# Head-by-head k-v products on array halves, weight pairs in three pieces, and a second buffer for the last weight chunk

## Chip, core and metric

The kernel runs on one core of a Trainium2 chip. The metric is the device time of one launch in microseconds (us). Engines are named as in the profile: PE is TensorE's matrix products and PEld its weight loads, DVE is VectorE, ACT is ScalarE, POOL is GpSimd, SP is the engine whose queue issues every DMA of this kernel.

## What is computed

Linear attention without a softmax, an RMS norm by head, a gated two-matrix layer, and a second layer with softmax gating and a layer norm:

```python
kv = einsum('bhsd,bhse->bhde', k, v)            # b 4, h 8, s 576, d 64
out = einsum('bhsd,bhde->bhse', q, kv)
x = out / sqrt(mean(out * out, -1) + 1e-6) * g_norm       # -> 2304 x 512
g = (x @ w_a) * (x @ w_b)                                 # 512 -> 1536
y = g @ w_out                                             # 1536 -> 512
h = y @ w_in                                              # 512 -> 1024
solu = h * softmax(h)
out = layernorm(solu) * g_ln @ w_out2                     # 1024 -> 512
```

The weights arrive as 64-bit floats and are turned into pairs of 32-bit values (an upper and a lower half) on the chip.

## The kernel before

One Python program writes out the order of every engine's instructions: a planner (`Order`) keeps a clock per engine with fixed costs, and at each step the main loop picks what PE does next from what the plan says is ready. The costs (`od.pe(1.09, ...)`, `t_act`, `t_vec`, `tt`) decide order only. `tt` ("VG") goes to DVE or POOL, whichever the plan says ends first. DMAs are issued by SP in program order, so a DMA that waits for a buffer holds back all later ones.

**Attention** (`front`, `back`). For each batch b and pair of heads p, `att_kv` multiplies k and v over the 576 tokens: four products of 128 rows and one tail of 64 rows, each 128 x 128, though only the two 64 x 64 blocks on the diagonal (one for each head) are used. ACT copies these into `bd`. The k-v buffers are two (`R_KV`), so the load of pair p + 2 waits for pair p's products. `att_1` multiplies q by `bd`, and DVE, ACT and POOL scale it. `att_2` transposes a tile of 128 tokens (line 785) and multiplies it by the constant matrices `m1`, `m2` (line 809), which give the sums and differences of token halves and rows that the next stage needs. Tokens are in three groups g of 2 x 288, 2 x 416 and 2 x 448; groups 0 and 1 pass through line 809, and group 2 gets its sums later in `third_group`.

**The two products x @ w_a and x @ w_b** (`Set`, line 926). For each of 12 chunks f of 128 columns and each group g, seven products of block sums (`PROD`, in the order `SEQ`) replace eight (Strassen-Winograd), each of 6 instructions on upper and lower halves. A chunk's weights go through `decode` (five DVE operations on two buffers), `gather`, `sums` into the stage buffer `wst` (part of `mx`; one buffer, `R_ST`), and `make_w`: ACT casts the upper half into `aw` (line 548), and DVE or POOL subtracts to get the lower half (line 270, as all of `tt`). There are two `aw` slots (`R_W`). `make_w` works in two pieces, 512 columns (rows 0 and 1 of the seven, for P1 and P2) and 1280 (all others). Chunks from 2 on are decoded only after `third_group` is done (`EARLY`). The last two chunks run groups 0 and 1 first: (10,0), (10,1), (11,0), (11,1), then (10,2), (11,2). Between them the 12 chunks of w_out and later matrices ("late" chunks) are decoded too; 11 of these are put away in DRAM meanwhile (`IN_AB`).

**The rest** (lines 1110 to 1154): g @ w_out, then h, the softmax and layer norm, and the last product.

Of the kernel before, what the change touches and what calls it, by code (L numbers as in the profile page):

```python
# [9 lines left out]
F32 = mybir.dt.float32  # L10
# [13 lines left out]
NF1 = DF1 // P  # L24
# [3 lines left out]
SC = 4  # L28
# [31 lines left out]

PROD = {"P1": (0, 1), "P2": (1, 2), "P3": (6, 0), "P4": (3, 6), "P5": (4, 4), "P6": (5, 5), "P7": (2, 3)}
SEQ = ["P1", "P2", "P6", "P5", "P7", "P4", "P3"]
NOP = 7
IN_AB = 11
EARLY = 2
# [126 lines left out]
def attention_moe_moe_kernel(ctx: ExitStack, tc, kv_in, kv_tail, q_in, g_norm, w1, w_in, w_out2, g_ln, out):  # L194
# [3 lines left out]
    nc = tc.nc  # L198
# [8 lines left out]
    att = tc.alloc_tile_pool(name="att", bufs=1, side="left")  # L207
# [83 lines left out]
    mix = {}  # L291
    for n in (P, D):
        c = n // 2
        m1, m2 = (att.tile([P, 4, c], F32, tag=f"m{n}_{i}", name=f"m{n}_{i}") for i in range(2))
        i0, i1 = ident[:, 0:c], ident[:, c:2 * c]
        nc.vector.memset(m2, 0.0)
        nc.vector.tensor_copy(out=m1[:, 0], in_=i0)
        for r in (1, 3):
            nc.vector.tensor_tensor(out=m1[:, r], in0=i0, in1=i1, op=ALU.subtract)
        for d in (m1[:, 2], m2[:, 3]):  # L300
            nc.vector.tensor_tensor(out=d, in0=i1, in1=i0, op=ALU.subtract)
        nc.vector.tensor_tensor(out=m2[:, 0], in0=m2[:, 1], in1=i0, op=ALU.subtract)
        nc.vector.tensor_copy(out=m2[:, 2], in_=i0)
# [31 lines left out]
    n_load, n_late = [0, 0], [0]  # L335
# [30 lines left out]
    def can(r, k):  # L366
        return pick(r, k) is not None
# [46 lines left out]
    def decode_more():  # L414

        q, lq = dec_q
        while q and q[0] in arrived and can(R_UF, q[0]):
            k = q[0]
            if k[1] not in stage:
                if k[1] >= EARLY and not third[1] or not R_ST.ok():  # L420
                    break
                stage[k[1]] = [R_ST.take(), wst, 2]
            decode(q.pop(0))
        for k in list(lq):
            if k in arrived and can(R_UF, k) and (own() or place(k) is not None):
                lq.remove(k)
                decode(k)
# [97 lines left out]
    def make_w():  # L525

        while w_wait and R_W.ok():
            f, st = w_wait.pop(0)
            slot = w_at[f] = R_W.take()
            hi, lo = w_ops(slot % 2)  # L530
            src = st[1]
            rank = rank_of(("w", f, 0)) - 0.2
            w_left[f] = NG
            left = [2]
            for half in range(2):
                s = slice(512, WSZ) if half else slice(0, 512)
# [15 lines left out]

    left_of = {}
    def w_used(f):
        w_left[f] -= 1
        if not w_left[f]:
            R_W.give(w_at[f])
            for h in range(2):
                w_ready.pop((f, h))
            make_w()  # L560

    half = {}
# [90 lines left out]
    tiles = {(b, i): (n, g, c) for b, i, n, g, c in AT}  # L653
# [22 lines left out]
    def run_front():  # L676
        w, b, i = front.pop(0)
        if w == "kv":
            od.pe(1.09, lambda: att_kv(b, i))
        else:  # L680
            od.pe(0.88, lambda: att_1(b, i))

    def run_back():
        _, b, t, x, sx = back.pop(0)
        od.pe(0.44 if tiles[b, t][1] == 2 else 2.0, lambda: att_2(b, t, x, sx))

    def att_kv(b, p):
        (slot, t, _), tl = arrived.pop(("kv", b, p)), arrived["tail", b, 0][1]
        sp = R_PA.take()
        bank, ps = ps_tile()  # L690
        o = ps[:, 0:P]
        for c in range(SC):
            nc.tensor.matmul(  # L693
                o, lhsT=t[:, c * P:(c + 1) * P], rhs=t[:, (SC + c) * P:(SC + c + 1) * P], start=c == 0, stop=False
            )
        r0 = D * (p % 2)
        nc.tensor.matmul(
            o, lhsT=tl[r0:r0 + D, p // 2, 0:P], rhs=tl[r0:r0 + D, p // 2, P:2 * P], start=False, stop=True
        )
        bd = bds[b % 2, p]  # L700

        def done(t):
            R_PA.give(sp)
            bd_ready[b, p] = t

        od.chain([
            ("A", 0.25, lambda: nc.scalar.copy(out=bd[0:D, 0:D], in_=ps[0:D, 0:D])),
            ("A", 0.25, lambda: nc.scalar.copy(out=bd[D:P, D:P], in_=ps[D:P, D:P])),
            ps_done(bank),
            (None, 0, done),  # L710
        ], rank=b, t=od.now + 1.09 + 0.2)
# [46 lines left out]
    def t_sums(s, d):  # L758

        c = s.shape[-1]  # L760
        return [
            ("V", t_vec(4 * c), lambda: nc.vector.tensor_tensor(
                out=d[:, 0:4].rearrange("p (a k) c -> p a k c", k=2),
                in0=s[:, 0:2].unsqueeze(1).to_broadcast([P, 2, 2, c]),
                in1=s[:, 2:6].rearrange("p (a k) c -> p a k c", k=2), op=ALU.subtract)),
            ("V", t_vec(2 * c), lambda: nc.vector.tensor_tensor(
                out=d[:, 4:6], in0=s[:, 2:4], in1=d[:, 2:4], op=ALU.subtract)),
            ("V", t_vec(2 * c), lambda: nc.vector.tensor_tensor(
                out=d[:, 6:8], in0=s[:, 6:8], in1=d[:, 4:6], op=ALU.subtract)),
        ]  # L770

    def pair_ops(hi, lo, src):
# [4 lines left out]
    def att_2(b, t, x, sx):  # L777
        n, g, c0 = tiles[b, t]
        c = n // 2
        sp = R_PA.take()  # L780
        bank, ps = ps_tile()
# [5 lines left out]
        rank = 1 + b  # L787
# [33 lines left out]
        for bk, src, h, l, m, dt in (  # L821
# [20 lines left out]
    third = [False, False]  # L842
# [48 lines left out]
    class Set:  # L891
# [14 lines left out]
        def run(s):  # L906
# [371 lines left out]
    while order or sets:  # L1278
# [21 lines left out]
        if not now and order and len(sets) < (1 if att_left[0] else ACTIVE):  # L1300
            s = Set(*order[0])
# [4 lines left out]
        if now:  # L1306
            s = now[0]
# [17 lines left out]
    while todo_o:  # L1325
# [94 lines left out]
```

## Time and profile before

| | |
|---|---|
| median of 3 runs | 759.5 us (758.02 to 759.54) |
| profiled execution | 757.83 us, its span 755.9 us |
| PE busy | 720.0 us, 95% of the span |
| DVE, POOL, ACT busy | 485.9, 302.7, 256.4 us |
| mean granted TensorE clock | 0.989 |

PE's busy time is modelled up to the end of each product, so it is not the share of its best speed. A granted clock of 1.00 is 2.4 GHz and 0.50 is 1.2 GHz. The rows further down are whole lines of the profile; "x8" counts instructions, and one 32-bit product is two of them.

### The profile page before, as it was taken

Reading aid. Unit: us, or ns where it says so; the run is one execution under the profiler, and the core shown is the slowest. Engines: PE = TensorE matmul, PEld = TensorE weight load, DVE = VectorE, ACT = ScalarE, POOL = GpSimd, SP = SyncE. Lnnn points to the kernel's source line nnn. Section 1 sums busy time; section 2 is a strip of 40 time slices with the busy share of each in tenths; the row PEclk is TensorE's granted clock in tenths of the full one; section 3 lists DMA queues with packets and bytes.
Section 4 is the critical chain, followed back from the end, with each engine's and each line's share of the span. In section 5 each row is a group of like instructions: output and inputs, shape, how many; then the busy total and the mean of one; then the engine's idle time right before and its main releaser. Section 6 shows DMA issues by size and latency. Waiting matters only on the chain.

```text
span 755.9 us, 10032 instructions
## 1 busy us (share of the span) xinstructions
PE 720.0 (95%) x3760; PEld 635.0 (84%) x3760; DVE 485.9 (64%) x726; ACT 256.4 (34%) x446; POOL 302.7 (40%) x287
## 2 busy tenths in 40 slices
PE   6989999799999999997989999999999999999997
PEld 5888898799899999897977788788888888988886
DVE  2857668989998899985586989733340165055361
ACT  1434554332433423432334444322232123213222
POOL 0454555654555544654167752612213222120110
PEclk9979999999999999999999999999999999999999
DMA  7165501443444534431878561211112101200101
GB/s 246 72 254 175 188 16 51 156 160 116 158 172 150 174 126 146 161 143 39 294 272 287 167 204 62 70 42 43 55 42 71 49 15 43 63 1 14 29 15 42
DMA packets 36336, 86.64 MB, mean 115 GB/s; under 512 B 4416, under 2 KB 12352, under 8 KB 36288
## 3 DMA queue, kind: packets, MB, share of 16 engines
q1 hardware_dynamic: 36288, 86.00, 33.8%
q8 instruction: 29, 0.48, 0.2%
q14 instruction: 19, 0.16, 0.1%
HBM read 61.35 MB, written 24.64 MB: 114 GB/s over the span
## 4 chain that ended last, share of the span: by engine, by line
PE 79%; DVE 9%; DMA 3%; POOL 3%; issue 2%; ACT 2%; SPq 0%; POOLq 0%; DVEq 0%; ACTq 0%
PE ps L926 26%; PE ps L1152 9%; PE ps L1154 9%; PE ps L1153 9%; PE ps L1110 5%; PE ps L1111 5%; PE ps L1112 5%; PE ps L809 3%; PE ps L723 3%; PE ps L693 2%; PE ps L1227 2%; PE ps L785 1%; POOL mx L270 1%; DVE mx L460 1%; DMA kv<-in_kv 1%
## 5 line engine op out<-in xcount | busy, mean ns | idle before, releaser
L926 PE MATMUL ps<-a,aw 128*128 128x288 f32 (+2 forms) x1512 | 274.3, 341 | 14.7 <-POOL aw L270 7.9
L926 PEld LDWEIGHTS ps<-a,aw 128*128 128x128 f32 x1512 | 256.6, 189 | 30.2 <-POOL aw L270 8.6
L270 POOL TENSOR_TENSOR gy<-mx,gy 128x512 fp32r<-128x512 f32 (+1 forms) x43 | 50.0, 1163 | 96.4 <-ACT gy L1081 93.0
L1198 DVE TENSOR_REDUCE mx<-ps 128x1 f32<-128x1024 f32 x18 | 22.0, 1221 | 82.5 <-PE ps L1154 82.3
L1110 PE MATMUL ps<-gy,a 128*128 128x512 f32 (+1 forms) x192 | 70.9, 369 | 2.3 <-DVE aw L1136 1.4
L1111 PE MATMUL ps<-gy,a 128*128 128x512 f32 (+1 forms) x192 | 69.7, 363 | 0.0
L1112 PE MATMUL ps<-gy,a 128*128 128x512 f32 (+1 forms) x192 | 69.7, 363 | 0.0
L944 ACT COPY gg<-ps 128x288 f32<-128x288 f32 (+2 forms) x72 | 34.4, 479 | 101.4 <-PE ps L926 97.8
L1152 PE MATMUL ps<-a,aw 128*128 128x512 f32 (+1 forms) x178 | 67.9, 381 | 0.0
L1153 PE MATMUL ps<-a,aw 128*128 128x512 f32 (+1 forms) x178 | 67.8, 381 | 0.0
L1154 PE MATMUL ps<-a,aw 128*128 128x512 f32 (+1 forms) x178 | 67.8, 381 | 0.0
L1000 POOL TENSOR_TENSOR gg<-gg,t 128x288 f32<-128x288 f32 (+2 forms) x36 | 41.4, 1150 | 58.0 <-DVE gg L998 57.9
L270 POOL TENSOR_TENSOR mx<-mx 128x512 f32<-128x512 f32 (+2 forms) x45 | 57.7, 1287 | 6.5 <-DVE mx L270 2.0
L751 POOL TENSOR_TENSOR r<-r,mhalf 128x8 f32<-128x8 f32 (+1 forms) x20 | 34.5, 1734 | 50.8 <-DVE r L740 50.6
L270 POOL TENSOR_TENSOR mx<-f,u 128x512 f32<-128x512 f32 x24 | 31.8, 1327 | 49.8 <-DVE u L469 48.5
L1081 ACT CAST gy<-mx 128x512 fp32r<-128x512 f32 (+1 forms) x48 | 27.2, 568 | 67.0 <-PE ps L1112 54.8
L1237 DVE TENSOR_TENSOR aw<-ps,aw 128x1024 fp32r<-128x1024 f32 x13 | 15.9, 1224 | 44.3 <-ACT aw L1236 44.2
L1199 ACT ACTIVATE mx<-ps,mx 128x1024 f32<-128x1024 f32 x18 | 20.1, 1118 | 69.0 <-DVE mx L1198 69.0
L1110 PEld LDWEIGHTS ps<-gy,a 128*128 128x128 f32 x192 | 36.3, 189 | 8.4 <-DVE aw L1136 1.8
L1112 PEld LDWEIGHTS ps<-gy,a 128*128 128x128 f32 x192 | 36.2, 189 | 5.7
L1111 PEld LDWEIGHTS ps<-gy,a 128*128 128x128 f32 x192 | 36.3, 189 | 5.3
L1152 PE MATMUL ps<-a 128*128 128x512 f32 x99 | 38.8, 392 | 1.3 <-DVE a L1237 1.3
(120 smaller groups left out, 1307.4 us busy)
## 6 DMA issues: line engine op xcount, KB each, us to landing
raw<-in_w SPq DMA_DIRECT2D x25, 512.0 KB, 4.2
mx<-gd SPq DMA_DIRECT2D x48, 256.0 KB, 2.7
kv<-in_kv SPq DMA_DIRECT2D x16, 512.0 KB, 3.3
mx<-in_w SPq DMA_DIRECT2D x11, 512.0 KB, 3.4
lscw<-mx SPq DMA_DIRECT2D x11, 512.0 KB, 2.6
a<-lscw SPq DMA_DIRECT2D x11, 512.0 KB, 6.8
gd<-gg SPq DMA_DIRECT2D x12, 448.0 KB, 2.5
gd<-gg SPq DMA_DIRECT2D x12, 416.0 KB, 3.0
```

The lines of the kernel that those rows point to most:

```text
L270: lambda e=e: e.tensor_tensor(out=out, in0=in0, in1=in1, op=op) for e in (nc.vector, nc.gpsimd)))
L751: ("G", 1.75, lambda: nc.gpsimd.tensor_tensor(out=r[0:n], in0=r[0:n], in1=mhalf[0:n], op=ALU.pow)),
L926: nc.tensor.matmul(o, lhsT=a[:, k], rhs=b[:, kt], start=first and kt == m == 0, stop=kt == 1 and m == 2, skip_group_check=not first,)
L944: od.chain([("A", t_act(s.n, True), lambda: nc.scalar.copy(out=dst(), in_=ps)), (None, 0, done)], t=t)
L1000: ("G", t_pool(s.n), lambda: nc.gpsimd.tensor_tensor(out=d, in0=d, in1=t3, op=ALU.mult)),
L1081: ("A", t_act(n), lambda t=t, gh=gh: nc.scalar.copy(out=gh, in_=t)),
L1110: nc.tensor.matmul(o, lhsT=wh[:, s], rhs=gh, start=f == 0, stop=False)
L1111: nc.tensor.matmul(o, lhsT=wh[:, s], rhs=gl, start=False, stop=False)
L1112: nc.tensor.matmul(o, lhsT=wl[:, s], rhs=gh, start=False, stop=f == NF1 - 1)
L1152: nc.tensor.matmul(o, lhsT=ah, rhs=bh, start=first, stop=False)
L1153: nc.tensor.matmul(o, lhsT=ah, rhs=bl, start=False, stop=False)
L1154: nc.tensor.matmul(o, lhsT=al, rhs=bh, start=False, stop=last)
```

## The change

`att_kv` makes the products head by head: 64 columns of k as weights and 64 of v, head 0 into partitions 0 to 63 (the left half of the array's columns) and head 1 into partitions 64 to 127, in turn: 10 products of 64 x 64 in the place of 5 of 128 x 128 (the two blocks that nobody read are no longer made); each head's sum stands in the columns 0 to 63 of the bank. `m2` loses its row of zeros (four blocks become three), for which the rows of the sums are numbered anew. `make_w` works in three pieces of 512, 768 and 512 columns, each with its own flag. Where the stage buffer is taken, the last chunk (11) may use another part of `mx`, if 11 late chunks have been started and the buffers that lie there are free. The planner's cost of a k-v product goes from 1.09 to 0.75, that of `att_2` from 2.0 to 1.9.

```diff
-PROD = {... "P4": (3, 6), "P5": (4, 4), "P6": (5, 5), "P7": (2, 3)}
+PROD = {... "P4": (3, 5), "P5": (4, 6), "P6": (5, 4), "P7": (2, 3)}
...
-        m1, m2 = (att.tile([P, 4, c], F32, tag=f"m{n}_{i}", name=f"m{n}_{i}") for i in range(2))
+        m1, m2 = (att.tile([P, 4 - i, c], F32, tag=f"m{n}_{i}", name=f"m{n}_{i}") for i in range(2))
...
-                if k[1] >= EARLY and not third[1] or not R_ST.ok():
+                if k[1] >= EARLY and not third[1]:
                     break
-                stage[k[1]] = [R_ST.take(), wst, 2]
+                if R_ST.ok():
+                    stage[k[1]] = [R_ST.take(), wst, 2]
+                elif k[1] == NF1 - 1 and n_late[0] >= IN_AB and R_RAW.ok(2) and R_UF.ok(2) and R_UF.ok(3):
+                    R_RAW.take(2), R_UF.take(2), R_UF.take(3)
+                    stage[k[1]] = [None, mx[:, 1792:3584], 2]
+                else:
+                    break
...
-            for half in range(2):
-                s = slice(512, WSZ) if half else slice(0, 512)
+            for half, s in enumerate((slice(0, 512), slice(1024, WSZ), slice(512, 1024))):
...
-        o = ps[:, 0:P]
-        for c in range(SC):
-            nc.tensor.matmul(
-                o, lhsT=t[:, c * P:(c + 1) * P], rhs=t[:, (SC + c) * P:(SC + c + 1) * P], start=c == 0, stop=False
-            )
...
+        for c in range(SC + 1):
+            for h in range(2):
+                o = ps[h * D:(h + 1) * D, 0:D]
+                if c < SC:
+                    k, v = (t[:, x * P + h * D:x * P + (h + 1) * D] for x in (c, SC + c))
+                else:
+                    k, v = (tl[r0:r0 + D, p // 2, x * P + h * D:x * P + (h + 1) * D] for x in range(2))
+                nc.tensor.matmul(o, lhsT=k, rhs=v, start=c == 0, stop=c == SC)
...
-                o = pt[:, kt * 4 * c:(kt + 1) * 4 * c]
...
+                o = pt[:, kt * 4 * c:kt * 4 * c + m.shape[-1]]
...
-            half = 0 if p in ("P1", "P2") else 1
+            half = {"P1": 0, "P2": 0, "P6": 1, "P5": 1}.get(p, 2)
```

The order moves on all engines up to the end of the line 926 stage; behind it PE's order is unchanged. Two places follow. In the names, `gg1_2` is the result tile of chunk 1 and group 2, `t31_2` its third buffer, `aw_80` the finished weights, `mx` the stage and late buffers. Lines of the changed kernel are shifted (457 to 475 were 451 to 469, 965 to 1008 were 957 to 1000).

The first place is the start of chunk 2. DVE before:

```order
L985 TENSOR_TENSOR gg1_2_1035<-ps_94,gg1_2_1035 128x448
L270 TENSOR_TENSOR mx_144<-mx_144 128x2x256
L998 TENSOR_TENSOR gg1_2_1035<-ps_94,gg1_2_1035 128x448
L460 SCALAR_TENSOR_TENSOR mx_144<-mx_144 128x512
L465 TENSOR_SCALAR mx_144<-mx_144 128x512
L469 SCALAR_TENSOR_TENSOR mx_144<-mx_144 128x512
L270 TENSOR_TENSOR aw_80<-mx_144,aw_80 128x1280
```

DVE now, at the same place:

```order
L270 TENSOR_TENSOR mx_142<-mx_142 128x256
L466 SCALAR_TENSOR_TENSOR mx_142<-mx_142 128x512
L471 TENSOR_SCALAR mx_142<-mx_142 128x512
L986 TENSOR_TENSOR t31_2_1213<-ps_94,t31_2_1213 128x448
L475 SCALAR_TENSOR_TENSOR mx_142<-mx_142 128x512
L993 TENSOR_TENSOR gg1_2_1139<-ps_94,gg1_2_1139 128x448
L1006 TENSOR_TENSOR gg1_2_1139<-ps_94,gg1_2_1139 128x448
L270 TENSOR_TENSOR aw_80<-mx_142,aw_80 128x512
L270 TENSOR_TENSOR aw_80<-mx_142,aw_80 128x768
```

The lower half of the first piece (512 columns), which POOL made before (its rows are not shown), now stands on DVE, behind the last two sums of set (1,2) and behind a late chunk's operations.

The second place is the start of chunk 11 on POOL. Before:

```order
L270 TENSOR_TENSOR mx_144<-mx_144 128x256
L270 TENSOR_TENSOR mx_144<-mx_144 128x2x256
L270 TENSOR_TENSOR mx_144<-mx_144 128x256
L1000 TENSOR_TENSOR gg10_1_2771<-gg10_1_2771,t310_1_2841 128x416
L270 TENSOR_TENSOR aw_80<-mx_144,aw_80 128x512
L1000 TENSOR_TENSOR gg11_0_2867<-gg11_0_2867,t311_0_2922 128x288
```

POOL now:

```order
L270 TENSOR_TENSOR mx_142<-f0_147,u0_145 128x512
L270 TENSOR_TENSOR mx_142<-f1_148,u1_146 128x512
L1008 TENSOR_TENSOR gg9_2_2751<-gg9_2_2751,t39_2_2844 128x448
L270 TENSOR_TENSOR mx_142<-mx_142 128x256
L270 TENSOR_TENSOR aw_80<-mx_142,aw_80 128x512
L1008 TENSOR_TENSOR gg10_0_2820<-gg10_0_2820,t310_0_2895 128x288
L270 TENSOR_TENSOR aw_80<-mx_142,aw_80 128x512
L1008 TENSOR_TENSOR gg10_1_2888<-gg10_1_2888,t310_1_2964 128x416
```

Chunk 11's gathers, sums and lower halves stood behind the end of (10,1); they now stand around the end of (9,2) and ahead of the end of (10,1).

## Rows read from the trace of the kernel before

**Rows 1.** The page: busy time by engine; the chain that ended last, by engine.

```profile
PE 720.0 (95%) x3760; PEld 635.0 (84%) x3760; DVE 485.9 (64%) x726; ACT 256.4 (34%) x446; POOL 302.7 (40%) x287
PE 79%; DVE 9%; DMA 3%; POOL 3%; issue 2%; ACT 2%; SPq 0%; POOLq 0%; DVEq 0%; ACTq 0%
```

**Rows 2.** Waits of PE: us in total, times, longest.

```profile
PE ps L926 <- POOL aw L270: 7.9, 3, 3.8
PE ps L926 <- DVE aw L270: 1.4, 2, 1.1
```

**Rows 3.** Timeline, first 24 us: start, us, engine, instruction, [idle before <- releaser].

```profile
1.65 4.84 SPq L352 DMA_DIRECT2D kv<-in_kv  x2
4.05 2.08 PE L693 MATMUL ps<-kv 128*128 128x128 f32 x8 [4.05 <-DMA kv<-in_kv]
6.78 2.07 PE L693 MATMUL ps<-kv 128*128 128x128 f32 x8
18.45 5.58 PE L723 MATMUL ps<-bd,q 128*128 128x128 f32 x28 [1.04 <-DMA q<-in_q]
```

**Rows 4.** Windows: length, busy PE, PEld, DVE, ACT, POOL, clock, DMA share, GB/s.

```profile
0.00:10.00 10.00, 5.95 (x22) 5.05 (x23) 3.00 (x24) 2.06 (x5) 0.72 (x7) 1.00 0.54 188
10.00:20.00 10.00, 8.07 (x30) 6.43 (x30) 2.78 (x4) 1.53 (x7) 0.00 (x0) 1.00 0.92 323
40.00:50.00 10.00, 10.00 (x44) 9.10 (x44) 1.32 (x4) 3.80 (x9) 4.60 (x5) 0.50 0.96 360
50.00:60.00 10.00, 9.46 (x67) 8.60 (x66) 8.66 (x16) 4.67 (x11) 4.34 (x3) 1.00 0.20 77
60.00:70.00 10.00, 10.00 (x68) 9.06 (x67) 8.82 (x18) 3.73 (x10) 4.24 (x4) 1.00 0.75 262
```

**Rows 5.** Timeline, PE around a later k-v product and a transpose of 64 columns.

```profile
87.43 1.06 PE L693 MATMUL ps<-kv 128*128 128x128 f32 x8
88.42 0.48 PE L697 MATMUL ps<-tail 64*128 64x128 f32 x2
88.83 0.66 PE L785 MATMUL ps<-ident,x 128*128 128x128 f32 x4
...
98.08 0.46 PE L785 MATMUL ps<-ident,x 64*128 64x64 f32 x4
98.47 1.06 PE L926 MATMUL ps<-a,aw 128*128 128x288 f32 x6
```

**Rows 6.** The chain that ended last, from 28 to 47 us: start, us, what.

```profile
28.17 1.73 PE ps L809 x8
...
36.36 3.25 DMA kv<-in_kv
...
39.75 1.96 PE ps L693 x8
...
44.67 2.00 PE ps L693 x8
```

**Rows 7.** Timeline, the start of chunk 2.

```profile
143.74 0.61 DVE L998 TENSOR_TENSOR gg<-ps,gg 128x448 f32<-128x448 f32 x1
...
146.11 1.45 POOL L270 TENSOR_TENSOR aw<-mx,aw 128x512 fp32r<-128x512 f32 x1
146.47 1.63 DVE L469 SCALAR_TENSOR_TENSOR mx<-mx 128x512 f32<-128x512 uint32 x1
...
147.61 12.60 PE L926 MATMUL ps<-a,aw 128*128 128x288 f32 x69 [3.83 <-POOL aw L270]
```

**Rows 8.** Windows (columns as in the windows above) at the start of chunk 2.

```profile
144.00:148.00 4.00, 0.39 (x3) 0.39 (x4) 3.93 (x4) 1.78 (x2) 4.00 (x4) 1.00 0.56 218
...
150.00:152.00 2.00, 2.00 (x8) 1.95 (x8) 2.00 (x4) 0.68 (x2) 1.75 (x1) 0.50 0.38 152
```

**Rows 9.** Groups by line and form: DVE's lower half of 512 columns, xcount | busy, mean ns.

```profile
L270 DVE TENSOR_TENSOR aw<-mx,aw 128x512 fp32r<-128x512 f32 x4 | 4.7, 1179 | 0.6 <-ACT aw L548 0.6
```

**Rows 10.** Timeline, the start of chunk 11.

```profile
351.80 8.45 PE L926 MATMUL ps<-a,aw 128*128 128x288 f32 x54 [3.22 <-POOL aw L270]
```

More of the change, by code (lines that the diff above doesn't have):

```diff
@@ L53 @@
 YB = [(0, 512), (512, 512), (1024, 512), (1536, 512), (2048, 256)]
-PROD = {"P1": (0, 1), "P2": (1, 2), "P3": (6, 0), "P4": (3, 6), "P5": (4, 4), "P6": (5, 5), "P7": (2, 3)}
+PROD = {"P1": (0, 1), "P2": (1, 2), "P3": (6, 0), "P4": (3, 5), "P5": (4, 6), "P6": (5, 4), "P7": (2, 3)}
 SEQ = ["P1", "P2", "P6", "P5", "P7", "P4", "P3"]
@@ L293, in attention_moe_moe_kernel @@
         c = n // 2
-        m1, m2 = (att.tile([P, 4, c], F32, tag=f"m{n}_{i}", name=f"m{n}_{i}") for i in range(2))
+        m1, m2 = (att.tile([P, 4 - i, c], F32, tag=f"m{n}_{i}", name=f"m{n}_{i}") for i in range(2))
         i0, i1 = ident[:, 0:c], ident[:, c:2 * c]
-        nc.vector.memset(m2, 0.0)
         nc.vector.tensor_copy(out=m1[:, 0], in_=i0)
-        for r in (1, 3):
-            nc.vector.tensor_tensor(out=m1[:, r], in0=i0, in1=i1, op=ALU.subtract)
-        for d in (m1[:, 2], m2[:, 3]):
+        for d in (m1[:, 2], m1[:, 3]):
+            nc.vector.tensor_tensor(out=d, in0=i0, in1=i1, op=ALU.subtract)
+        for d in (m1[:, 1], m2[:, 2]):
             nc.vector.tensor_tensor(out=d, in0=i1, in1=i0, op=ALU.subtract)
-        nc.vector.tensor_tensor(out=m2[:, 0], in0=m2[:, 1], in1=i0, op=ALU.subtract)
-        nc.vector.tensor_copy(out=m2[:, 2], in_=i0)
+        nc.vector.tensor_scalar(out=m2[:, 0], in0=i0, scalar1=-1.0, scalar2=None, op0=ALU.mult)
+        nc.vector.tensor_copy(out=m2[:, 1], in_=i0)
         mix[n] = tuple(x.rearrange("p r c -> p (r c)") for x in (m1, m2))
@@ L533, in make_w @@
             w_left[f] = NG
-            left = [2]
-            for half in range(2):
-                s = slice(512, WSZ) if half else slice(0, 512)
+            for half, s in enumerate((slice(0, 512), slice(1024, WSZ), slice(512, 1024))):
                 n, x = s.stop - s.start, src[:, s]
@@ L542, in done @@
                     if not left_of[f]:
-                        R_ST.give(st[0])
+                        if st[0] is None:
+                            R_RAW.give(2), R_UF.give(2), R_UF.give(3)
+                        else:
+                            R_ST.give(st[0])
                         decode_more()
-                left_of[f] = 2
+                left_of[f] = 3
                 od.chain([
@@ L557, in w_used @@
             R_W.give(w_at[f])
-            for h in range(2):
+            for h in range(3):
                 w_ready.pop((f, h))
@@ L678, in run_front @@
         if w == "kv":
-            od.pe(1.09, lambda: att_kv(b, i))
+            od.pe(0.75, lambda: att_kv(b, i))
         else:
@@ L684, in run_back @@
         _, b, t, x, sx = back.pop(0)
-        od.pe(0.44 if tiles[b, t][1] == 2 else 2.0, lambda: att_2(b, t, x, sx))
+        od.pe(0.44 if tiles[b, t][1] == 2 else 1.9, lambda: att_2(b, t, x, sx))
     def att_kv(b, p):
@@ L690, in att_kv @@
         bank, ps = ps_tile()
-        o = ps[:, 0:P]
-        for c in range(SC):
-            nc.tensor.matmul(
-                o, lhsT=t[:, c * P:(c + 1) * P], rhs=t[:, (SC + c) * P:(SC + c + 1) * P], start=c == 0, stop=False
-            )
-        r0 = D * (p % 2)
-        nc.tensor.matmul(
-            o, lhsT=tl[r0:r0 + D, p // 2, 0:P], rhs=tl[r0:r0 + D, p // 2, P:2 * P], start=False, stop=True
-        )
+        r0 = D * (p % 2)
+        for c in range(SC + 1):
[3 more added lines that the diff above has]
+                    k, v = (t[:, x * P + h * D:x * P + (h + 1) * D] for x in (c, SC + c))
+                else:
+                    k, v = (tl[r0:r0 + D, p // 2, x * P + h * D:x * P + (h + 1) * D] for x in range(2))
+                nc.tensor.matmul(o, lhsT=k, rhs=v, start=c == 0, stop=c == SC)
         bd = bds[b % 2, p]
@@ L707, in att_kv @@
             ("A", 0.25, lambda: nc.scalar.copy(out=bd[0:D, 0:D], in_=ps[0:D, 0:D])),
-            ("A", 0.25, lambda: nc.scalar.copy(out=bd[D:P, D:P], in_=ps[D:P, D:P])),
+            ("A", 0.25, lambda: nc.scalar.copy(out=bd[D:P, D:P], in_=ps[D:P, 0:D])),
             ps_done(bank),
             (None, 0, done),
-        ], rank=b, t=od.now + 1.09 + 0.2)
+        ], rank=b, t=od.now + 0.75 + 0.2)
         R_KV.give(slot)
@@ L762, in t_sums @@
             ("V", t_vec(4 * c), lambda: nc.vector.tensor_tensor(
-                out=d[:, 0:4].rearrange("p (a k) c -> p a k c", k=2),
+                out=d.rearrange("p (a k) c -> p a k c", k=2)[:, 0:4:3],
                 in0=s[:, 0:2].unsqueeze(1).to_broadcast([P, 2, 2, c]),
@@ L766, in t_sums @@
             ("V", t_vec(2 * c), lambda: nc.vector.tensor_tensor(
-                out=d[:, 4:6], in0=s[:, 2:4], in1=d[:, 2:4], op=ALU.subtract)),
+                out=d[:, 2:4], in0=s[:, 2:4], in1=d[:, 6:8], op=ALU.subtract)),
             ("V", t_vec(2 * c), lambda: nc.vector.tensor_tensor(
-                out=d[:, 6:8], in0=s[:, 6:8], in1=d[:, 4:6], op=ALU.subtract)),
+                out=d[:, 4:6], in0=s[:, 6:8], in1=d[:, 2:4], op=ALU.subtract)),
         ]
```

## The prediction

> **What bounds the kernel.** I read the page first. PE is busy for 95% of the span, and the chain that ended last runs on PE for 79% of its length, with DVE, DMA and POOL sharing most of the rest [rows 1]. So a microsecond taken from PE is a microsecond gained only where PE is what ends last. The edits touch four places, and each has its own limit.
>
> The first 25 us belong to DMA. PE's first product waits 4.05 us for the first load, and at 18.45 it waits once more for q [rows 3]. The DMA engines are busy for 0.54 of the first 10 us and 0.92 of the next 10 [rows 4]. The early products are also slow: eight instructions take 2.08 us [rows 3], and the same eight take 1.06 us later [rows 5].
>
> Between 28 and 48 us the chain goes from PE to a load of k and v of 3.25 us, and back to k-v products of 1.96 and 2.00 us [rows 6]. The granted clock is 0.50 (1.2 GHz) from 40 to 50 [rows 4]. From 50 to 70 PE is busy again for nearly all the time, but DVE is busy for 8.66 and 8.82 us of each 10, so here two engines are near their limit [rows 4].
>
> In the stage of line 926, PE's waits for the lower half of the weights sum to 7.9 us on POOL (three, the longest 3.8) and 1.4 us on DVE [rows 2]. Two of them are large: 3.83 us before chunk 2 [rows 7] and 3.22 us before chunk 11 [rows 10].
>
> **The k-v product itself.** A product before is eight instructions of 128 columns and two for the tail. From the start at 87.43 to the next shape at 88.83 it takes 1.40 us [rows 5]. Line 809 gives a clean price: eight instructions of 256 columns in 1.73 us [rows 6], 0.216 each, 0.00084 us a column. So 128 columns cost 0.108 and 64 columns 0.054, both estimates. Eight of 128 make 0.86, and the tail starts at 88.42, 0.99 after the first; 0.13 is the switch to another shape. The tail's two make 0.22, and the next shape starts 0.41 later; 0.19 is the switch back [rows 5].
>
> After, a product is 20 instructions of 64 columns (16 and 4), in turn on the left and right half of the array. Nothing in this trace shows two halves at work together, so I bound it. If they work fully beside each other, it is 10 x 0.054 = 0.54, and with the switches, which grow to some 0.45 because the array is split, 0.99. If one follows the other, it is 20 x 0.054 + 0.45 = 1.53. If each costs what a transpose of 64 columns does, (98.47 - 98.08 - 0.13) / 4 = 0.065 [rows 5], it is 1.75. I take w = 1.10: nearly beside each other, with 0.11 for the first and last pieces, since the two halves write different partitions and need no result of each other. That saves 0.30 us at 2.4 GHz and 0.60 at 1.2 GHz.
>
> One rule speaks against this edit. The Trainium skill, page "TensorEngine Tiling (Array Packing)", section "Key Properties", says that changing the tiling mode drains the engine; the trace agrees, 0.13 and 0.19 at the two shape switches [rows 5]. The same section says that different tiles can load weights and multiply in parallel, which no run here shows yet; by it alone the product would be 0.99 and the sum below 1.7 us lower.
>
> Where these savings count:
>
> (a) Batch 0. The loads of pairs 2 and 3 wait for the buffers of pairs 0 and 1, so a shorter product lets SP issue them, and q behind them, sooner; DMA has room in the first 10 us (0.54) and PE waits for q at 18.45 [rows 3, 4]. Two products at the slow speed count: -1.2. Pairs 2 and 3 themselves lie behind their loads: 0.
>
> (b) Batch 1. Its first product stands ahead of the load of 3.25 in the chain (-0.3), and two stand in the chain at the clock of 0.50 [rows 4, 6]: -1.2. Together -1.5.
>
> (c) Batches 2 and 3. Eight products at 0.30 are 2.4. DVE is busy 87 and 88% there [rows 4]; I count 0.8 of it, -1.9.
>
> So a change of w weighs 2 x 2 + 1 + 2 x 2 + 8 x 0.8 = 15.4 times.
>
> **att_2.** Of the eight instructions of line 809, four go from 256 to 192 columns: 4 x 64 x 0.00084 = 0.216 us a tile. Four tiles of batch 0 stand in the chain [rows 6]: -0.86. Later six whole tiles and a half make 1.4; with the 0.8 of (c), -1.1. The setup of m2 loses a few DVE operations that lie under the first load's 4.05 us [rows 3]: 0, and a few tenths of a us if that cover went.
>
> **Start of chunk 2.** Before, POOL makes the lower half of the first piece from 146.11 to 147.56, and PE starts at 147.61 [rows 7]. Now DVE makes it, behind a late chunk's last decode operation and the last two sums of set (1,2), and DVE is already full: busy 3.93 of the 4 us from 144 to 148 [rows 8]. Before, DVE's last decode operation ended at 148.10 (146.47 + 1.63) [rows 7]. The two sums that stood ahead of it (0.61 each, as line 998) have moved behind it, another sum of 0.61 has moved in: 148.10 - 1.22 + 0.61 = 147.5. Then come the two sums, 1.22, and the lower half, 1.18 [rows 9]: 149.9, against 147.56. That is **+2.3**. If the planner's shift lets the earlier operations run sooner it is 0; if the six PE products that now precede the last results delay the sums, +3.5. The clock falls to 0.50 behind this wait before [rows 8] and should again, so that adds nothing. The other pieces (768, 512) come later than PE needs the first, and P1 and P2 use only the first.
>
> **Start of chunk 11.** The wait of 3.22 us [rows 10] stands there because the stage buffer is freed late, and then gathers, sums and lower half follow on POOL. With a second buffer they stand ahead of the end of (10,1), so only a normal gap stays: **-3.1**. At worst (the buffer's old users finish late) it is 0.
>
> **Other chunk starts.** The waits that remain, 7.9 + 1.4 - 3.83 - 3.22 = 2.25 us [rows 2], may go or grow; I take 0, and 1.5 either way. The 12 more casts and subtractions (three pieces for two) lie beside PE: ACT is busy 34%, POOL 40% [rows 1]. Behind the stage of line 926 PE's order is the same: 0.
>
> **The sum.** -1.2 - 1.5 - 1.9 - 0.86 - 1.1 + 2.3 - 3.1 = -7.4 us. The profiled execution took 757.83, so it would be 750.4; the median lies 1.7 above the profiled one, at 759.5, and I predict for a median **752.1**.
>
> **Rivals.** (R1) *The halves go one after another.* For it: no row shows them together, and the weights of each piece must be loaded as well (PEld is busy 84% [rows 1]). Against it: they share neither columns nor output partitions. Then w = 1.53, +0.13 x 15.4 = +2.0, and the other terms are -0.86 - 1.1 + 2.3 - 3.1 = -2.8: together -0.8, 758.7, no change that can be told.
>
> (R2) *DVE bounds the attention from 50 to 100 us.* For it: 8.66 and 8.82 of 10 [rows 4]; PE would only wait longer for the normalised tiles. Against it: PE itself has no idle time from 60 to 70. Then (c) and the later att_2 are worth nothing, 3.0 less: -4.4, 755.1.
>
> (R3, the other side) *Small pieces cost a fixed time.* For it: the transposes of 64 columns at 0.065 each [rows 5], while 64 columns should take 0.054. Against it: a transpose also waits for its operand. With w = 1.75 the k-v products cost +0.35 x 15.4 = +5.4, and with -2.8 it is +2.6: 762.1, slower. It decides (slower by 1.5 us) from w = 1.40 + (1.5 + 2.8) / 15.4 = 1.68, that is from 0.061 us a piece. Beside it, in a sentence by itself: the Trainium skill, page "TensorEngine Tiling (Array Packing)", section "Instruction Overhead", says that a product of one column takes as long as one of 60 and that no tiling should cut a dimension that is already small; 64 columns stand just above that, and no run here shows the floor.
>
> **How the numbers follow.** Forecast 0.57, R1 0.17, R2 0.16, R3 0.10. A measurement of this kernel can tell about 0.2% (1.5 us) from no change, so the forecast and R2 are faster, and with a part of R1, at its faster end, that is 0.79; the rest of R1 is the same, 0.11; R3 is slower, 0.10. The likeliest case alone has 746 to 756: w = 0.99 (-1.7), chunk 2 without loss (-2.3) and other starts (-1.5) towards one end, chunk 2 at +3.5 and other starts at +1.5 with a part of chunk 11's gain lost towards the other. The range runs from 745, a little below that, up to 759.5, which takes in R2 and R1 and leaves out R3.
>
> **What the profile will show.** If I am right, a k-v product at 2.4 GHz takes about 1.1 us to the next shape; the load of pair 2 of batch 0 is issued earlier and line 723 starts earlier than 18.45; line 809's groups take about 1.5 us; PE waits some 6 us before chunk 2, for DVE; and no wait of over 1 us stands before chunk 11. R1 shows as 1.5 us for the product, R3 as 1.7 or more, R2 as new idle time of PE between 50 and 100 with DVE as what ended it. The prediction fails if the shorter k-v work leaves PE with more idle time early and the granted clock stays at 0.50 for longer than from 40 to 50 [rows 4], or if the new piece order makes PE wait at chunk starts that had no wait before.

## Result and the profile after

The changed kernel is slower: a median of 767.9 us against 759.0, a ratio of 1.0111 with a 95% interval of 1.0063 to 1.0159. The forecast was 752.1, faster. The profiled execution took 767.73 us.

First the page of the changed kernel, the line that answers to [rows 1]:

```profile
PE 713.2 (93%) x3920; PEld 626.5 (82%) x3920; DVE 485.5 (63%) x725; ACT 258.3 (34%) x458; POOL 314.1 (41%) x298
```

PE has 6.8 us less work shown and the span is 9.7 us longer: the time is in waits. PE's waits, as in [rows 2], the largest:

```profile
PE ps L707 <- DMA kv<-in_kv: 11.4, 6, 4.0
PE ps L934 <- DVE t L986: 8.6, 9, 2.3
PE ps L934 <- ACT a L783: 4.8, 1, 4.8
...
PE ps L934 <- DVE aw L270: 1.9, 1, 1.9
...
PE ps L934 <- POOL aw L270: 1.4, 2, 1.0
```

Line 926 is now 934. What it waited for before, the lower half of the weights, has shrunk from 9.3 us to 3.3; in its place stand one wait of 4.8 us for the third group of tokens (line 783) and nine for a sum on DVE (line 986, which adds a product into `t`).

The edited products, in PE's timeline (the places of [rows 3] and [rows 5]):

```profile
4.05 1.12 PE L707 MATMUL ps<-kv 128*64 128x64 f32 x16 [4.05 <-DMA kv<-in_kv]
...
17.93 6.81 PE L731 MATMUL ps<-bd,q 128*128 128x128 f32 x30 [1.21 <-DMA q<-in_q]
...
28.25 1.68 PE L817 MATMUL ps<-m,x 128*128 128x256 f32 x8
29.76 0.60 PE L793 MATMUL ps<-ident,x 128*128 128x128 f32 x4
...
52.46 0.69 PE L707 MATMUL ps<-kv 128*64 128x64 f32 x16
53.07 0.33 PE L707 MATMUL ps<-tail 64*64 64x64 f32 x4
53.33 1.16 PE L731 MATMUL ps<-bd,q 128*128 128x128 f32 x8
```

A k-v product at 2.4 GHz takes 53.33 - 52.46 = 0.87 us to the next shape, where 1.40 stood before; the eight instructions of att_2 (now line 817) take 1.51 in place of 1.73. So both edits of the attention did on PE what they should, the first even more.

PE's timeline behind the attention, the places of [rows 7] and [rows 10] among it:

```profile
106.40 0.46 PE L793 MATMUL ps<-ident,x 64*128 64x64 f32 x4
106.79 14.02 PE L934 MATMUL ps<-a,aw 128*128 128x416 f32 x72
125.60 0.74 PE L934 MATMUL ps<-a,aw 128*128 128x448 f32 x1 [4.80 <-ACT a L783]
...
147.30 19.71 PE L934 MATMUL ps<-a,aw 128*128 128x288 f32 x112 [1.88 <-DVE aw L270]
...
245.17 15.84 PE L934 MATMUL ps<-a,aw 128*128 128x448 f32 x84 [2.31 <-DVE t L986]
...
295.62 9.25 PE L934 MATMUL ps<-a,aw 128*128 128x448 f32 x48 [1.89 <-DVE t L986]
...
329.43 57.58 PE L934 MATMUL ps<-a,aw 128*128 128x288 f32 x318 [0.30 <-DVE t L986]
```

The wait before chunk 11 is gone (PE runs from 329 to 387 us without a gap that shows). Chunk 2 starts at 147.30, where it did before (147.61), though the last transpose started 5.1 us earlier, at 106.40 in place of 111.51:

```profile
111.51 0.46 PE L785 MATMUL ps<-ident,x 64*128 64x64 f32 x4
```

And the windows around the wait for the third group (columns as in [rows 4]):

```profile
118.00:122.00 4.00, 2.81 (x15) 2.32 (x13) 3.97 (x6) 0.91 (x1) 2.01 (x2) 1.00 0.27 94
122.00:126.00 4.00, 0.40 (x1) 0.29 (x1) 3.00 (x5) 1.41 (x3) 3.40 (x2) 0.63 0.04 12
126.00:130.00 4.00, 3.52 (x10) 2.90 (x10) 4.00 (x7) 1.18 (x3) 0.00 (x0) 0.52 0.73 242
```

Behind the wait the granted clock is about one half (1.2 GHz) up to 130 us. Over the whole execution the mean granted clock is 0.982 against 0.989 before; e1 below has 0.980 and is the faster kernel, so the clock alone does not make the loss.

Where the time went, from PE's timeline of each profiled execution (us):

| kernel | last transpose starts | chunk 2 starts | line 1110's products start | from chunk 2 to there |
|---|---|---|---|---|
| before | 111.5 | 147.6 | 383.4 | 235.8 |
| changed | 106.4 | 147.3 | 391.5 | 244.2 |
| e1 front, old order | 107.5 | 143.6 | 381.3 | 237.7 |
| e2 front, new costs | 104.3 | 145.6 | 390.2 | 244.6 |
| e3 three pieces alone | 108.7 | 144.9 | 389.3 | 244.4 |
| e5 all, old costs | 103.7 | 139.6 | 384.8 | 245.1 |
| e9 all, order of four products | 107.1 | 144.0 | 385.5 | 241.5 |
| e13 front, new costs, that order | 104.7 | 142.3 | 381.9 | 239.6 |

Chunk 2 "starts" here with the first product that needs the lower half of its weights. Each row is one execution: the last transpose stands at 107.1 and 107.4 in e4 and e7, which have the changed kernel's order up to there, and at 106.0 in e8, which has e1's, so a us or so in this column says nothing. The changed kernel loses 8.1 us up to line 1110's products and 1.6 behind them, where its granted clock is 0.93 from 390 to 405 us and 0.96 from 405 to 420 and was 1.00 before.

### The profile page after: what moved, and what is told of

Same layout as the page of the kernel before. It is cut to its first block, busy times and chain, and to the rows that moved or that the text cites. A ratio compares the mean times of both kernels' runs of the same rounds, so it can differ in the third digit from the quotient of the medians.

```text
span 765.6 us, 10399 instructions
## 1 busy us (share of the span) xinstructions
PE 713.2 (93%) x3920; PEld 626.5 (82%) x3920; DVE 485.5 (63%) x725; ACT 258.3 (34%) x458; POOL 314.1 (41%) x298
## 4 chain that ended last, share of the span: by engine, by line
PE 51%; DVE 3%; issue 1%; ACT 1%; POOL 0%; DVEq 0%; ACTq 0%; POOLq 0%
PE ps L1160 9%; PE ps L1162 9%; PE ps L1161 9%; PE ps L934 6%; PE ps L1118 6%; PE ps L1119 6%; PE ps L1120 6%; PE ps L1235 2%; DVE a L270 1%; DVE ps L460 1%; DVE f L466 1%; DVE ps L457 0%; DVE ps L471 0%; ACT a L1089 0%; DVE u L475 0%
## 5 line engine op out<-in xcount | busy, mean ns | idle before, releaser
L934 PE MATMUL ps<-a,aw 128*128 128x416 f32 (+2 forms) x1512 | 282.4, 346 | 22.5 <-DVE t L986 8.6
L934 PEld LDWEIGHTS ps<-a,aw 128*128 128x128 f32 x1512 | 260.6, 192 | 41.3 <-DVE t L986 12.5
L270 POOL TENSOR_TENSOR mx<-mx 128x256 f32<-128x256 f32 (+2 forms) x45 | 53.1, 1184 | 9.6 <-DVE mx L475 2.8
L759 POOL TENSOR_TENSOR r<-r,mhalf 128x8 f32<-128x8 f32 (+1 forms) x20 | 32.7, 1642 | 45.7 <-DVE r L748 45.6
L457 DVE TENSOR_SCALAR ps<-ps 128x512 f32<-128x512 f32 x41 | 27.9, 689 | 19.6 <-ACT ps L454 19.6
```

The lines of the kernel that those rows point to most:

```text
L270: lambda e=e: e.tensor_tensor(out=out, in0=in0, in1=in1, op=op) for e in (nc.vector, nc.gpsimd)))
L457: nc.vector.tensor_scalar(out=v, in0=v, scalar1=WMIN, scalar2=WMAX, op0=ALU.max, op1=ALU.min)
L759: ("G", 1.75, lambda: nc.gpsimd.tensor_tensor(out=r[0:n], in0=r[0:n], in1=mhalf[0:n], op=ALU.pow)),
L934: nc.tensor.matmul(o, lhsT=a[:, k], rhs=b[:, kt], start=first and kt == m == 0, stop=kt == 1 and m == 2, skip_group_check=not first,)
```

## The experiments

Ratios are to the kernel before, run on the same chip. "The front" is the k-v products by head and the narrow m2.

**e1, the front in the old order.** The planner keeps 1.09 and 2.0, so the order of work stays; weights in two pieces, one stage buffer.

```diff
-        od.pe(0.75, lambda: att_kv(b, i))
+        od.pe(1.09, lambda: att_kv(b, i))
...
-        od.pe(0.44 if tiles[b, t][1] == 2 else 1.9, lambda: att_2(b, t, x, sx))
+        od.pe(0.44 if tiles[b, t][1] == 2 else 2.0, lambda: att_2(b, t, x, sx))
...
-        ], rank=b, t=od.now + 0.75 + 0.2)
+        ], rank=b, t=od.now + 1.09 + 0.2)
```

> The kernel before with the k-v products by head and the narrower m2, the planner's costs left as they were, so that every engine keeps the order of before. Theory A (the k-v products and m2 did gain, and the loss comes from the new order of the weight work in the line 926 stage): faster than before; the products of this kernel save 0.4 us each at 2.4 GHz, some 4 to 6 us on PE up to the last transpose, of which the third group's work on DVE and the wait before chunk 2 let 1 to 4 us through: 755 to 758 us. Theory B (less PE work early costs clock or puts the waits elsewhere, whatever the order): no gain or slower, 759 to 764 us.

754.9 us, 0.9952 (0.9930 to 0.9973): faster. The two edits of the attention gain when the order stays: chunk 2 starts 4.0 us earlier than before, behind the same wait (3.82 us).

**e2, the front with the planner's new costs** (0.75 and 1.9).

> As the run with the old order, but with the planner's new costs for the k-v product and att_2 (0.75, 1.9); the weights still come in two pieces, one stage buffer. Theory A with the pieces as the cause: as the old order within 3 us, 754 to 759 us. Theory C (the planner's new costs alone make the worse order): about as slow as the whole change, 764 to 770 us.

762.6 us, 1.0067 (1.0043 to 1.0091): slower. The same instructions in another order cost some 8 us more than e1. Its two longest waits of PE behind the attention are 4.77 us for the third group, where e1 waits 0.38, and 5.69 before chunk 11, where e1 waits 3.20.

**e3, three pieces alone**, on the kernel before.

```diff
-            for half in range(2):
-                s = slice(512, WSZ) if half else slice(0, 512)
+            for half, s in enumerate((slice(0, 512), slice(1024, WSZ), slice(512, 1024))):
```

> The kernel before with the weights in three pieces alone. Theory A with the pieces as the cause: slower than before by 5 to 10 us, 764 to 769 us, with more lower halves on POOL and PE's waits for DVE's sums as in the changed kernel. Theory C: as before within 2 us, 757 to 761 us.

764.3 us, 1.0075 (1.0049 to 1.0102): slower. PE's largest waits behind the start of chunk 2:

```profile
286.88 17.63 PE L924 MATMUL ps<-a,aw 128*128 128x288 f32 x94 [2.13 <-POOL aw L270]
...
356.14 29.94 PE L924 MATMUL ps<-a,aw 128*128 128x288 f32 x154 [3.94 <-POOL aw L270]
```

The second is the wait before chunk 11 again; the first, at the same place for the same reason, was 0.83 us before. The pieces have changed the order too: PE's order of the seven products by set differs from the order before from chunk 2 on.

**e4, the change without the second buffer.**

> The changed kernel without the second buffer for chunk 11. If the second buffer gained what was forecast (3.1 us at the start of chunk 11) it is slower than the changed kernel, 770 to 772 us. If the earlier work on chunk 11 is what makes DVE late from 285 us on (theory D), it is faster than the changed kernel by 3 to 6 us, 762 to 765 us.

768.5 us, 1.0130 (1.0087 to 1.0173): not to be told from the change. Its longest wait behind 330 us is 1.02 us, so in this order there is no wait before chunk 11 to be gained. Neither theory's number came.

**e5, the whole change with the planner's old costs** (1.09 and 2.0, as in e1).

> The whole change, but with the planner's costs of before for the k-v product and att_2 (1.09 and 2.0). If what the pieces cost (5.8 us, measured alone) and what the new costs cost (7.7 us, measured in two pieces) are separate losses, this is the gain of the front in the old order (754.9 us) plus the pieces: 759 to 762 us. If the pieces alone make the loss in any order once PE is faster early: 766 to 769 us, as the whole change.

756.1 us, 0.9993 (0.9973 to 1.0013): as before the change. By the ratios the pieces cost some 3 us on top of e1 here, and the new costs 9 on top of e5. PE's order of the seven products is e3's here. In this order the second buffer is never taken, since its condition is not met when chunk 11 is decoded.

**e6, the change with the products of 128 columns back**, in the order of the change.

> The changed kernel with the k-v products of 128 columns back, in the order of the changed kernel (the planner still counts 0.75). The products cost some 0.45 us more each at 2.4 GHz, 1.2 in the first 15 us. If the lead of the shorter products is lost in the wait of 4.8 us for the third group's work on DVE and ACT, it costs nothing: 766 to 770 us. If the lead is passed on to the end: 4 to 7 us slower, 772 to 775 us.

769.0 us, 1.0157 (1.0119 to 1.0196), against 1.0111 (1.0063 to 1.0159) with the short products: not to be told from it. The timeline has the old price:

```profile
50.94 1.16 PE L700 MATMUL ps<-kv 128*128 128x128 f32 x8 [0.48 <-DVE gg L964]
52.02 0.49 PE L704 MATMUL ps<-tail 64*128 64x128 f32 x2
52.44 1.16 PE L730 MATMUL ps<-bd,q 128*128 128x128 f32 x8
```

So in the order of the change most of what the products save turns into waits: PE's gaps of over 0.15 us between the first load and the last transpose sum to 6.3 us with the wide products and to 15.3 with the short ones (the wait for the first load not counted). The last transpose starts at 107.14 with the wide products, which lies within the 106.40 to 107.42 of the three executions with the short ones: no lead is left to be seen.

**e7, filling the wait for the third group.** 26 products more ahead of the first product of set (0,2); their result is overwritten.

```diff
+            fill = {(0, 2): (0, 1, 26)}.get((f, g)) if p == "P1" else None
+            for j in range(fill[2] if fill else 0):
+                fw, fx = w_ops(w_at[fill[0]] % 2)[0], x_ops(fill[1])[0]
+                nc.tensor.matmul(s.A[1][:, 0:GN[fill[1]]], lhsT=fw[:, 0:P], rhs=fx[:, j % 2], start=True, stop=True)
```

> The changed kernel with 26 products of 128 x 416 put in (their result is overwritten) where PE waits 4.8 us before the first product of group 2, so that PE is busy there; the order of all other engines is the same. If the clock of 0.50 behind that wait (123 to 130 us) is what makes the sums of set (0,2) late, and through DVE's order the last decode step of chunk 2, the clock stays at 1.00 there and chunk 2 starts 2 to 3 us earlier: 764.5 to 766.5 us. If the wait itself or DVE's amount of work sets chunk 2's start, no change: 767 to 769 us.

773.5 us, 1.0204 (1.0166 to 1.0242): 6 us slower than the change. I had put them four products too early:

```profile
116.93 5.06 PE L933 MATMUL ps<-a,aw 128*128 128x416 f32 x26
121.83 4.84 PE L938 MATMUL ps<-a,aw 128*128 128x448 f32 x24
129.80 0.47 PE L938 MATMUL ps<-a,aw 128*128 128x448 f32 x1 [3.13 <-ACT a L783]
```

The 5.06 us did not come out of the wait: it only fell from 4.80 to 3.13, and its end moved from 125.60 to 129.80 (1.0 us of this stood already at the last transpose). PE was not ahead of DVE there, it was also what DVE waited for: sums of sets stand between DVE's steps of the third group (below).

**e8, filling the waits before chunks 2 and 11** in e1's order, with 18 and 16 such products at the right places.

> The front in the old order (754.9 us) with such products put into the waits before chunk 2 (18 of them) and before chunk 11 (16), where the clock fell to 0.50 after each. If a busy PE keeps the clock, it gains half of the two stretches at 0.50, about 3.4 us: 750.5 to 753 us. If the clock falls anyway, or the products delay the start behind them, 754 to 757 us.

753.0 us, 0.9944 (0.9917 to 0.9971); not to be told from e1 by the ratios. The windows behind chunk 2's start, first e1, then e8:

```profile
144.00:148.00 4.00, 4.00 (x19) 3.94 (x18) 4.00 (x5) 1.58 (x4) 3.67 (x2) 0.57 0.39 146
```

```profile
142.00:146.00 4.00, 3.75 (x23) 3.50 (x24) 4.00 (x4) 2.01 (x5) 3.92 (x3) 1.00 0.55 198
146.00:150.00 4.00, 4.00 (x27) 3.97 (x26) 4.00 (x8) 1.40 (x4) 0.32 (x1) 1.00 0.35 135
```

The clock stays at 2.4 GHz when PE has worked through the wait. That holds behind all six filled waits of e8, e12 and e14 (1.00 each time). Behind the unfilled waits of over 1.8 us at the same two places in the other kernels (1.88 to 5.69 us) it fell to 0.50, with two exceptions, which stayed at 1.00: the 3.22 us before chunk 11 in the kernel before and the 1.88 us before chunk 2 in the changed one.

**e9, the order of four products.** The change, and P6 of set (0,2), which needs the whole third group, comes behind P1 and P2 of set (1,2), as in the order before.

```diff
+            if (s.f, s.g, p) == (0, 2, "P6") and ((1, 2) in order or any((x.f, x.g) == (1, 2) and x.i < 2 for x in sets)):
+                return INF
```

> The changed kernel with one rule more for PE's order: P6 of set (0,2), which needs the third group whole, comes only when P1 and P2 of set (1,2) have been given out, as in the order of before (the planner then orders what follows anew). If the order of these four products is what made PE wait 4.8 us there, the wait falls to 2.5 to 3 us and chunk 2 starts at about 145 us in place of 147.3: 763 to 767 us, if the rest of the stage is as in the changed kernel. If DVE's own work sets the start of chunk 2, it still starts at 147 us: 767 to 770 us.

759.5 us, 1.0017 (0.9996 to 1.0039): 7 to 8 us of the loss come back, more than expected. The profile has the place mended, and a wait of 3.36 behind it, before chunk 2:

```profile
126.37 0.47 PE L936 MATMUL ps<-a,aw 128*128 128x448 f32 x1 [0.77 <-ACT a L783]
...
143.97 21.23 PE L936 MATMUL ps<-a,aw 128*128 128x288 f32 x112 [3.36 <-DVE aw L270]
...
193.05 14.32 PE L936 MATMUL ps<-a,aw 128*128 128x448 f32 x84 [2.29 <-DVE t L988]
```

**e10 and e11, one new cost at a time**, two pieces: 0.75 alone, then 1.9 alone.

> The front (two pieces, one buffer) with the planner's new cost for the k-v product alone (0.75; att_2 stays at 2.0). The old costs gave 754.9 us, both new ones 762.6. If a smaller planned cost pulls the products of line 926 into the attention and so makes the loss, most of it is here: 760 to 763 us. If any disturbed order of the stage from chunk 2 on loses some us by chance, it can be anywhere from 755 to 765.

> The same with the new cost of att_2 alone (1.9; the k-v product stays at 1.09). By the first reading (a smaller planned cost of the k-v products makes the loss) 754 to 757 us, since this cost moves little. By the second (any disturbed order loses) 757 to 765 us.

759.4 us, 1.0013 (0.9994 to 1.0032), and 753.5 us, 0.9930 (0.9910 to 0.9950). By the ratios the k-v cost brings 4.6 of the 8.7 us between e1 and e2, and the other cost alone none; what orders cost does not add up. The first reading is nearer, the second not excluded. e11 leaves PE's order of the seven products as it was before, and PE waits 0.38 us for the third group; in e10 it waits 4.22:

```profile
124.68 0.74 PE L926 MATMUL ps<-a,aw 128*128 128x448 f32 x1 [4.22 <-ACT a L775]
```

In e10, though, P1 and P2 of set (1,2) stand ahead of P6 of (0,2), as before. So the wait comes with the new k-v cost (0.4 us in e1, e3, e5 and e11; 4.2 to 4.8 in the changed kernel, e2, e4, e6 and e10), and the order of the four products (e9) is not the only way to it.

**e12 and e14, a better kernel.** e8 with 24 products of zeros in the first waits for k, v and q; then the same on the order of e11.

> The front in the old order with the products put into the waits before chunks 2 and 11 (753 us), and 24 more fp32 products of zeros before the first loads of k and v and of q, so that PE is busy in the first 15 us, where its products run at the lower speed. If the early slow speed ends sooner when PE is busy, the products of q behind 16 us take 3.5 in place of 6 to 7 us: 749 to 751 us. If not, or if the loads decide there, 752 to 755 us.

> The front in two pieces with the new cost of att_2 alone (753.5 us) and the products that fill the waits in the first 15 us and before chunks 2 and 11 (1.3 to 3 us in the old order). If the fills gain the same here, 749.5 to 751.5 us; if the two gains are one and the same, 752 to 754 us.

751.8 us, 0.9910 (0.9886 to 0.9935), and 752.3 us, 0.9910 (0.9886 to 0.9933). Both beat the kernel before and the change. By the ratios e12 cannot be told from e8, nor e14 from e11; the sum of e11's gain and the fills' (0.9888) lies just inside e14's interval, so whether the two add stays open. The products of q behind 17 us still take 0.49, 0.65 and 4.46 us in e12, not 3.5 in all. The first k-v product after the fill (e12):

```profile
2.02 3.88 PE L692 MATMUL ps<-bd 128*128 128x128 f32 x20 [2.02 <-DVE bd L283]
5.84 0.69 PE L701 MATMUL ps<-kv 128*64 128x64 f32 x16
```

**e13, the order of e9 on the front alone** (two pieces, both new costs).

> The front with both new costs, in two pieces, with the rule that holds P6 of set (0,2) behind P1 and P2 of set (1,2). Without the rule it took 762.6 us; the whole change with the rule took 759.5. If the order of these products is also what the new costs broke in two pieces, and the pieces are what is left of the loss, this comes near the front in the old order: 754 to 757 us. If the new costs lose by the rest of the stage's order too, 758 to 762 us.

754.3 us, 0.9936 (0.9911 to 0.9960): the rule mends the two-piece kernel whole (e2: 1.0067). What is left between e13 and e9, 0.8% or 6 us, belongs to the three pieces and the second buffer, with the order that they bring.

## Why the prediction was wrong

**What was right.** att_2: 0.216 a tile was forecast and 0.22 measured. R1 and R3 are both out: a product needs 0.87 us, not 1.53 or 1.75. Its 16 pieces take 0.61 us, where one after another they would take 16 x 0.054 = 0.86 by the forecast's estimate, so the halves do work beside each other. w = 1.10 was too high by 0.23: beside the 0.54 for the pieces, 0.33 is left for switches, first and last pieces, and the forecast had 0.56. The wait before chunk 11 went, and DVE made chunk 2's first lower half, as forecast.

**The step that failed first: the sum took the order of before and added the pieces.** "I take 0, and 1.5 either way" for the other chunk starts is the term. An edit of a planned cost or of the pieces can make a new order from the attention to chunk 11 (all that were tried here did, but for e11's), and from chunk 2's start to line 1110's products the changed kernel needs 244.2 us in place of 235.8, though the 3.22 us before chunk 11 are gone: 8.4 us more, where the sum had 3.1 less for this stretch. e1, with the old order, shows the forecast's sign (-3.6 us); e2, the same work in the new order, is slower than before. That is shown; no rival of mine had it. The last sign of failing came nearest, more idle time early and longer at 0.50: PE's gaps up to the last transpose grew from 6.8 us to 15.3. But e1 has 12.6 there, and no higher clock, and is faster, so this alone does not make the change slower.

**The place with the longest wait.** The planner puts what is ready first by its own clock, and by that clock P6 of set (0,2), which needs the third group, could start at 113.6 us; on the chip the group was ready at 125.6. So in the new order it put P6 and P5 of this set ahead of P1 and P2 of (1,2), which need only its first part. PE's order, chunk.group and product:

```
before:  0.2 P2, 1.1 P4, 1.1 P3, 1.2 P1, 1.2 P2, 0.2 P6, 0.2 P5, 1.2 P6
changed: 1.1 P4, 1.1 P3, 0.2 P2, 0.2 P6, 0.2 P5, 1.2 P1, 0.2 P7, 1.2 P2
```

PE waits 4.80 us and then runs at the lower clock. What follows is DVE's queue:

```profile
120.18 0.58 DVE L993 TENSOR_TENSOR gg<-ps,gg 128x416 f32<-128x416 f32 x1
120.68 0.37 DVE L776 TENSOR_TENSOR mx<-mx 128x224 f32<-128x224 f32 x1
...
122.85 1.73 DVE L776 TENSOR_TENSOR mx<-mx 128x224 f32<-128x224 f32 x1
125.58 1.09 DVE L270 TENSOR_TENSOR a<-mx,a 128x896 fp32r<-128x896 f32 x1 [1.00 <-ACT a L783]
...
130.18 1.28 DVE L471 TENSOR_SCALAR ps<-f 128x512 uint32<-128x512 uint32 x2
133.77 0.62 DVE L986 TENSOR_TENSOR t<-ps,t 128x448 f32<-128x448 f32 x1 [2.31 <-ACT t L952]
...
134.89 1.27 DVE L475 SCALAR_TENSOR_TENSOR u<-raw,ps 128x512 f32<-128x512 uint32 x2
```

The sum of line 986 waits 2.31 us for PE's slow products (for ACT's copy of one, line 952), and chunk 2's last decode step (line 475) stands behind it. So the lead of 5 us at the last transpose is gone when chunk 2 starts. e9 undoes this: chunk 2 starts 3.3 us earlier. The rest of its gain (4.1 of 7.4 us between the two profiled executions) lies behind chunk 2, where the rule made the planner order anew as well; how much of that is this place's late effect and how much a luckier order stays open. From the last transpose to chunk 2 the kernel before needs 36.1 us, e1 36.1, e9 36.9 and the changed kernel 40.9.

**Start of chunk 2, +2.3.** The engine was right: DVE's lower half ends last. But PE waits 1.88 us for it (3.36 in e9), not some 6, since PE itself came later; and the clock, which was to fall behind this wait as before, stayed at 1.00 there and fell behind the third group's. So +2.3 was the smaller part; in e5, in another order, POOL makes it and PE waits 3.7.

**The pieces.** The forecast hid them under "ACT 34%, POOL 40%". They cost 3 us (e5 against e1), 6 (e13 to e9, with the second buffer) and 5.8 (e3 alone). In e3 and e5 chunk 2 starts 2.7 and 4.0 us earlier than in the kernel before and in e1, and 8.6 and 7.4 us are lost between there and line 1110. No run has three pieces in the old order, so how much of this is the order and how much the pieces' own work stays open. The groups by form show what moved, first the changed kernel, then e13:

```profile
L270 POOL TENSOR_TENSOR aw<-mx,aw 128x512 fp32r<-128x512 f32 x18 | 27.7, 1545 | 6.1 <-ACT aw L555 6.0
...
L270 DVE TENSOR_TENSOR aw<-mx,aw 128x768 fp32r<-128x768 f32 x9 | 14.4, 1601 | 3.7 <-ACT aw L555 3.7
...
L270 POOL TENSOR_TENSOR aw<-mx,aw 128x768 fp32r<-128x768 f32 x3 | 6.4, 2135 | 0.1
```

```profile
L270 POOL TENSOR_TENSOR aw<-mx,aw 128x512 fp32r<-128x512 f32 x9 | 12.8, 1424 | 4.1 <-ACT aw L547 4.1
```

POOL makes 21 lower halves (34.1 us) in place of 9 (12.8 us); with the pieces alone, e3 has 23 (38.7 us) and the kernel before 9 (14.5 us). At PE's wait of 2.31 us in the changed kernel, DVE's queue, then POOL's:

```profile
240.87 2.05 DVE L270 TENSOR_TENSOR aw<-mx,aw 128x768 fp32r<-128x768 f32 x1
242.84 1.75 DVE L475 SCALAR_TENSOR_TENSOR mx<-mx 128x512 f32<-128x512 uint32 x1
244.51 0.61 DVE L986 TENSOR_TENSOR t<-ps,t 128x448 f32<-128x448 f32 x1
```

```profile
238.92 3.18 POOL L270 TENSOR_TENSOR aw<-mx,aw 128x512 fp32r<-128x512 f32 x2
242.05 1.98 POOL L270 TENSOR_TENSOR mx<-mx 128x512 f32<-128x512 f32 x1
```

The sum for which PE waits stands behind two DVE operations of 2.05 and 1.75 us, while POOL works all the time. Line 475 reads all its operands from `mx` here, in SBUF; in this trace the eleven of this form take 0.68 or 0.69 us or, seven of them, all while POOL works, 1.10 to 1.75; three of the other four stand beside POOL too. Those that read one operand from `ps` (as at 134.89) take 0.64 to 0.69 each, beside POOL or not. Line 776 shows the same: 0.37 us at 120.68, with POOL idle, and 1.73 at 122.85, beside this:

```profile
122.10 2.23 POOL L270 TENSOR_TENSOR a<-mx,a 128x896 fp32r<-128x896 f32 x1 [2.09 <-ACT a L783]
```

That POOL slows DVE is read from these rows, not tried by itself. The Trainium skill, page "SBUF — State Buffer", section "SBUF: two separate sides", says that a VectorE operation with two inputs in SBUF and a GpSimd operation that reads SBUF use a shared pair of ports, that whichever starts first holds it for its whole instruction, and that the other waits. These rows agree for operations that read two operands from there.

**The front, (a) to (c).** The weight of 15.4 was too high. With 0.53 saved in place of 0.30 it would give 8.2 us; e1 as a whole gained 3.6. In batch 0 DMA sets the pace, and shorter products only make longer gaps (six waits for k and v, 11.4 us in all, where there were two, 5.5 us in all): q's products start at 17.93 in place of 18.45, but 30 of them take 6.81 us, and line 793 follows at 25.80, later than before (25.34). e6 says the same of the changed order (9 us more gaps). So R2's thought, that others bound the attention, was right, with too small a chance, but DVE was the smaller part of it: PE's waits for DVE between 50 and 100 us grew from 1.5 to 2.7 us, those for the loads of k, v and q from 7.4 to 15.1.

**The second buffer, -3.1.** The wait went, but e4 has no such wait either in its order, and the two kernels cannot be told apart: the gain there is not shown, and is at most a few us.

## What to carry to other kernels

Where a planner with fixed costs writes the order, a changed cost is a change of the whole program: measure the edit with the order held (e1) before the order with the new cost (e2), and expect that the difference can be as large as the edit (8.7 us between e1 and e2, none with e11). Look at how far the plan's clock lies from the chip's at the places where an engine takes from two queues; a rule of one line there (e9, e13) was worth more than the products. A wait of PE is no slack when the engine that it waits for has PE's results in its own queue (e7).

## What was not expected of the hardware

Pieces of 64 columns, in turn on the two halves of the array's columns, take 0.61 / 16 = 0.038 us each, less than the estimate of 0.054 by columns: the halves overlap. On each half a piece has 0.076 us, more than 0.054, so either the overlap is not full or a piece has a fixed cost; no run here tells which. Behind most waits of 2 to 5 us the clock was at 1.2 GHz for a while (0.63 and 0.52 in the windows above), and it stayed at 2.4 when PE multiplied something useless through the wait (1.00 in e8). In the first 25 us products run at the lower speed while the windows give the clock as 1.00 (the trace's first record of it starts at 24 us in the changed kernel); with zeros multiplied from 2 us on, the first k-v product took 0.69 us for 16 pieces in place of 1.12.
